# Attention with rotary positions and a token and channel mixer: table loads on ScalarE's queue, the first pair's rotation in two parts with its first head written from PSUM, and 128-partition transposes of the tail rows

## The chip, the cores and the metric

The kernel runs on one core of a Trainium2 chip. The metric is the device time of one execution in microseconds. A core has five engines that run their own in-order queues: TensorE (PE; its weight loads are listed as PEld), VectorE (DVE), ScalarE (ACT), GpSimd (POOL) and SyncE (SP), the last of which issues the DMA transfers. PSUM is the memory that PE writes its results to.

## The reference

Inputs q, k and v are 4 x 8 x 576 x 64 in fp32 (batch, heads, positions, head width). Then come two mixers with residual sums.

```python
def rotate(x):
    x1, x2 = (x[..., :half], x[..., half:])
    return np.concatenate([x1 * cos - x2 * sin, x1 * sin + x2 * cos], axis=-1)
q_rot, k_rot = (rotate(q), rotate(k))
scores = scale * np.matmul(q_rot, k_rot.transpose(0, 1, 3, 2))
attn = softmax(scores)
x = concat_heads(np.matmul(attn, v))               # 4 x 576 x 512
h = np.maximum(x.T @ w_tok1, 0.0) @ w_tok2         # mixes the 576 positions, width 256
u = x + h.T
out = u + np.maximum(u @ w_ch1, 0.0) @ w_ch2       # mixes the 512 channels, width 1536
```

(softmax and concat_heads stand for the reference's lines.) The four weights are float64; the kernel converts them on the chip.

## The kernel before

**Number format.** A matmul takes operands in a format of fewer bits than fp32, so each operand is split into a high part (a copy that rounds, on ACT) and a low part (the fp32 value less the high part, on DVE or POOL), and a product is made of three passes: high by high, high by low, low by high. In attention the two parts of q are stacked on the 128 partitions (head width 64, twice), so that one matmul against the k high part that stands on both halves, and one against the k low part, give all of it.

**Attention.** The 32 combinations of batch and head go two heads at a time, as 16 pairs n. `prep(n)` (L245) makes a pair's operands: load k, q and v (`ld`, `ldt`, L254 to L259; 512 rows as 128 partitions of 4 rows, and the 64 tail rows as a fifth row R on 64 partitions); rotate k and q in four element-wise operations each (`rot`, L286 to L298: times sine, times cosine, and two half-width additions; pair 0 on DVE, the others on POOL); transpose on PE in two groups g into a PSUM tile (`tr`, L317 to L321: rows 0 and 1, then rows 2 and 3 and the tail, which is a 64 x 64 transpose at L321); copy the high part (`fh`, L325, ACT) and subtract the low part (`fl`, L328, DVE); and duplicate each head's parts on both partition halves by DMA over SP (`dup`, L340: eight for k, four for q). v is copied and split by two POOL operations (L272, L275). Four small POOL casts (L365) make a block-diagonal operand for the tail rows of q. The tables of cosines and sines are loaded in two halves over SP: the half for k first of all (L233), the half for q behind pair 0's k (L265).

`pair(n)` (L375) works off nine score tiles: four row tiles of head 0, the tail tile of both heads (L403), and four row tiles of head 1. For each: score matmuls (L412), the row maximum (L417, DVE), the exponential with its row sum (L427, ACT), transposes (L437 and L467, PE), their high parts (ACT, L442, L473) and low parts (DVE, L446, L476). After certain tiles nine matmuls with v follow (L491), and the two halves of the result are added (L494, L497). At a pair's end the result is transposed back (L524, L527) and scaled (L536, L543).

Beside this, `tok_weights` (L619) splits the token mixer's weights in six blocks through `f64_split` (L556): ACT makes a scaled absolute value and the low word's value (L576, L578), then a clamp (L580), a shift (L582), two mask operations (L584, L586), a product and a sum (L588, L590), the high part (L596) and the low part (L597). Clamp, product, sum and low part may go to DVE or POOL, whichever the planner thinks will end first; the rest of the integer work is DVE's.

**Mixers.** Once attention has ended, the token mixer (`tokens`, L668) runs for the four batches while seven blocks of the channel mixer's first weight group are split (`weights`, L732); then the channel mixer (L765, L789) runs four weight groups over six chunks of rows, and the next group's 7 blocks are split beside it.

**What sets the order.** No instruction is issued as it is written. Each is a task of class `Plan` (L56) with an engine, a modelled duration, the tasks that it depends on, the buffers that it takes, and a priority. `Plan.run` (L88) is a list scheduler: it keeps a modelled clock per engine, and of the tasks that can start earliest (within `SLACK`, L144, of the first) it takes the one with the lowest priority. The order in which tasks are picked is the order of each engine's queue on the chip, and it isn't changed there. Priorities are a position (9 n for pair n, plus the tile's number) plus an offset by kind of task out of `AT` (L143). The modelled durations are one-line formulas such as

```python
def pool1(n):
    return n * 0.00115 + 0.07
```

which is the clamp on POOL for n columns; on DVE the planner takes 0.0016 n + 0.05 for it.

Of the kernel before, what the change touches and what calls it, by code (L numbers as in the profile page):

```python
# [142 lines left out]
AT = {"qk": -21.76, "mx": 12.19, "ex": -0.31, "tr": 2.41, "eh": 3.13, "el": 11.77, "tt": -13.32, "th": -37.34, "tl": -11.54, "pv": -15.55, "p1": -1.22, "p2": -8.32, "fin": 13.39, "f6": 9.56, "load": -2.28, "rot": 8.1, "pt": -7.21, "dup": -7.81, "vs": -7.11}  # L143
SLACK = {"PE": 0.16, "ACT": 0, "DVE": 0.16, "POOL": 0, "SP": 0.46}  # L144
# [14 lines left out]
def pool1(n):  # L159
    return n * 0.00115 + 0.07  # L160
# [7 lines left out]
def rope_attention_mixer_kernel(ctx: ExitStack, tc: tile.TileContext, q, k, v, w_tok1, w_tok2, w_ch1, w_ch2, tab, out):  # L168
# [8 lines left out]
    nc = tc.nc  # L177
# [26 lines left out]
    def attention(ctx):  # L204
# [28 lines left out]
        nc.sync.dma_start(out=tabs[:, 0:2], in_=tab[0:2].rearrange("a p r d -> p a r d"))  # L233
# [11 lines left out]
        def prep(n):  # L245
            b, hp = divmod(n, HP)
            pos = 9 * n
            hb = {}
            for nm, src, pr in (("k", k, 0.0), ("q", q, 0.5), ("v", v, 1.0)):
# [14 lines left out]
                if nm == "k" and n == 0:  # L264
                    add("SP", 0.5, lambda: nc.sync.dma_start(out=tabs[:, 2:4], in_=tab[2:4].rearrange("a p r d -> p a r d")),  # L265
                        prio=pos + AT["load"])
                n5 = 2 * (R + 1) * D
                if nm == "v":
                    vb = Buf(vss)

                    def v1(e, rb=rb, vb=vb):
                        return lambda: e.tensor_copy(out=vb.t[:, :, :, 0:D], in_=rb.t.rearrange("p h r d -> p r h d"))  # L272

                    def v2(e, rb=rb, vb=vb):
                        return lambda: e.tensor_tensor(out=vb.t[:, :, :, D:2 * D], in0=rb.t.rearrange("p h r d -> p r h d"),  # L275
                                                       in1=vb.t[:, :, :, 0:D], op=ALU.subtract)

                    x = add("POOL", 0.74, v1(nc.gpsimd), l, [rb, vb], pos + AT["vs"])
# [7 lines left out]
                def rot(e, i, rb=rb, ub=ub, wb=wb, c=c):  # L286
                    def go():
                        src = rb.t.rearrange("p h r d -> p r h d")
                        bc = lambda j: tabs[:, j].unsqueeze(2).to_broadcast([P, R + 1, 2, D])
                        u, w = i and ub.t, i != 1 and wb.t  # L290
# [11 lines left out]
                for i in range(4):  # L302
                    w = n5 if i < 2 else n5 // 2
                    bufs = [[rb, wb], [rb, ub], [ub, wb], [ub, wb]][i]
                    if n == 0:
                        x = [add("DVE", dve(w), rot(nc.vector, i), x, bufs, pos + AT["rot"] + pr)]
                    else:
                        x = [add("POOL", pool(w), rot(nc.gpsimd, i), x, bufs, pos + AT["rot"] + pr)]
                hi, lo = Buf(hls[nm + "h"]), Buf(hls[nm + "l"])
                hb[nm] = (hi, lo)  # L310
                eh, el = [], []
                for g in range(2):
# [4 lines left out]
                    def tr(g=g, tb=tb, ub=ub):  # L317
                        for j, r in enumerate((0, 1) if g == 0 else (2, 3)):
                            nc.tensor.transpose(tb.t[:, j * P:(j + 1) * P], ub.t[:, r].rearrange("p h d -> p (h d)"), ident)  # L319
                        if g == 1:  # L320
                            nc.tensor.transpose(tb.t[:, 2 * P:2 * P + TL], ub.t[0:TL, R].rearrange("p h d -> p (h d)"),  # L321
                                                ident[0:TL, 0:TL])
# [8 lines left out]
                    x2 = add("PE", 0.15 * (2 + g) + 0.1 * g, tr, x, [tb, ub], pp)  # L331
# [12 lines left out]
                if nm == "k":  # L344
                    out_b = [Buf(khds), Buf(klds)]
                    done = {0: [], 1: []}
                    for h in range(2):
# [5 lines left out]
                else:  # L353
                    qb = Buf(qss)
                    done = {0: [], 1: []}
                    for h in range(2):
# [541 lines left out]
```

## Time and profile before

| | us |
|---|---|
| median of 3 runs (lowest to highest) | 728.04 (727.44 to 730.86) |
| the profiled execution | 726.98 |
| its span, from first to last instruction | 725.2 |
| PE busy | 667.1 (92% of the span) |
| DVE busy | 524.3 (72%) |
| ACT busy | 373.8 (52%) |
| POOL busy | 346.1 (48%) |

Busy time is summed over the records of an engine; matmuls are pipelined, so a busy PE is not PE at its peak. A group's line names the kernel's line, the engine, the operation, and its output and inputs by the names of the program's tiles without their numbers: `kh` and `kl` are k's high and low parts, `khd`, `kld` and `qs` the duplicated operands, `s` the scores, `p` the exponentials, `pt` their transposed parts, `t` a PSUM tile, `fa`, `fh` and `fc` the scratch of the weight split. Times in a timeline are microseconds from the span's start.

### The profile page before, as it was taken

How to read it: one execution, taken by the hardware profiler on the slowest of the kernel's cores; microseconds unless marked ns; L12 is line 12 of the kernel's file. 1: busy time of each engine (PE TensorE's matmuls, PEld its weight loads, DVE VectorE, ACT ScalarE, POOL GpSimd, SP SyncE). 2: the span in 40 equal slices, each digit the busy share in tenths (PEclk: the TensorE clock that was granted, in tenths of full speed). 3: DMA queues.
4: the chain of work that ended last, by engine and by line, in shares of the span. 5: the costliest groups of instructions: out<-in, count | busy, mean ns of one | idle time of the engine just before them, and what ended most of it. 6: DMA issues, size and time to landing. Idle time of an engine off the chain costs nothing.

```text
span 725.2 us, 11584 instructions
## 1 busy us (share of the span) xinstructions
PE 667.1 (92%) x3960; PEld 589.3 (81%) x3960; DVE 524.3 (72%) x919; ACT 373.8 (52%) x911; POOL 346.1 (48%) x352
## 2 busy tenths in 40 slices
PE   1698899999999999996948999999999999999997
PEld 0677788788889888885826898989899998989896
DVE  5799999999999999996897588644883375232322
ACT  2588889888888888884552253322431141101110
POOL 4899889788777777302880045121750161000000
PEclk9999999999999999997977999999999999999999
DMA  7575555545555555420220013011220010001122
GB/s 207 163 210 131 129 146 146 137 122 146 145 141 138 146 144 140 99 88 0 81 73 23 0 53 101 23 51 33 70 74 0 5 56 0 1 1 44 58 73 87
DMA packets 45914, 63.14 MB, mean 87 GB/s; under 512 B 13984, under 2 KB 27040, under 8 KB 45856
## 3 DMA queue, kind: packets, MB, share of 16 engines
q1 hardware_dynamic: 45856, 62.41, 31.9%
q8 instruction: 31, 0.51, 0.3%
q14 instruction: 27, 0.22, 0.1%
HBM read 30.41 MB, written 4.72 MB: 48 GB/s over the span
## 4 chain that ended last, share of the span: by engine, by line
PE 70%; DVE 13%; ACT 5%; POOL 4%; issue 4%; DMA 2%; SPq 1%; ACTq 0%; DVEq 0%; POOLq 0%
PE m L779 21%; PE m L802 21%; PE t L491 8%; PE s L412 6%; PE t L437 4%; PE m L717 3%; DVE nm L417 3%; DVE pt L446 2%; PE s L403 2%; ACT p L427 2%; PE t L319 1%; PE t L467 1%; PE m L695 1%; PE t L524 1%; DVE pt L476 1%
## 5 line engine op out<-in xcount | busy, mean ns | idle before, releaser
L781 ACT ACTIVATE gh<-m 128x384 fp32r<-128x384 f32 x72 | 35.3, 491 | 176.6 <-PE m L779 159.2
L427 ACT ACTIVATE p<-s,nm 128x576 f32<-128x576 f32 x144 | 108.0, 750 | 17.2 <-DVE nm L417 16.1
L417 DVE TENSOR_REDUCE nm<-s 128x1 f32<-128x576 f32 x144 | 107.7, 749 | 6.4 <-PE s L412 4.7
L446 DVE TENSOR_TENSOR pt<-t,pt 128x512 fp32r<-128x512 f32 (+1 forms) x160 | 97.3, 628 | 2.4 <-ACT pt L442 1.3
L779 PE MATMUL m<-uh,c1h 128*128 128x384 f32 x288 | 96.7, 336 | 0.0
L779 PE MATMUL m<-uh,c1l 128*128 128x384 f32 x288 | 96.6, 336 | 0.0
L779 PE MATMUL m<-ul,c1h 128*128 128x384 f32 x288 | 96.6, 335 | 0.0
L491 PE MATMUL t<-pt,vs 128*128 128x256 f32 (+1 forms) x576 | 88.7, 298 | 4.4 <-DVE pt L446 1.4
L783 DVE SCALAR_TENSOR_TENSOR gl<-m,gh 128x384 fp32r<-128x384 f32 x72 | 39.8, 556 | 70.7 <-ACT gh L781 70.6
L580 POOL TENSOR_SCALAR fa<-fa 128x512 f32<-128x512 f32 (+3 forms) x34 | 60.0, 1767 | 59.9 <-ACT fa L576 54.4
L491 PEld LDWEIGHTS t<-pt,vs 128*128 128x128 f32 x576 | 79.5, 188 | 8.5 <-ACT p L427 3.6
L437 PE MATMUL t<-ident,p 128*128 128x128 f32 x576 | 84.5, 277 | 1.9 <-DVE oT L497 0.7
L802 PE MATMUL m<-c2h,gl 128*128 128x512 f32 x216 | 85.1, 394 | 0.0
L802 PE MATMUL m<-c2l,gh 128*128 128x512 f32 x216 | 85.0, 393 | 0.0
L802 PE MATMUL m<-c2h,gh 128*128 128x512 f32 x216 | 84.8, 393 | 0.0
L442 ACT CAST pt<-t 128x512 fp32r<-128x512 f32 (+1 forms) x160 | 82.9, 550 | 3.4 <-PE t L437 2.1
L412 PE MATMUL s<-khd,qs 128*128 128x288 f32 x256 | 81.0, 332 | 3.3 <-ACT p L427 1.8
L804 DVE TENSOR_TENSOR X<-m,X 128x512 f32<-128x512 f32 x64 | 43.6, 688 | 49.4 <-PE m L802 49.4
L412 PE MATMUL s<-kld,qs 128*128 128x288 f32 x256 | 72.6, 298 | 0.0
L437 PEld LDWEIGHTS t<-ident,p 128*128 128x128 f32 x576 | 64.7, 140 | 8.5 <-DVE pt L446 2.5
L412 PEld LDWEIGHTS s<-khd,qs 128*128 128x128 f32 x256 | 48.9, 191 | 12.3 <-ACT p L427 9.1
L779 PEld LDWEIGHTS m<-ul,c1h 128*128 128x128 f32 x288 | 54.1, 188 | 0.9
(120 smaller groups left out, 1351.6 us busy)
## 6 DMA issues: line engine op xcount, KB each, us to landing
khd<-kh SPq DMA_DIRECT2D x64, 144.0 KB, 2.5
kld<-kl SPq DMA_DIRECT2D x64, 144.0 KB, 2.7
stg<-in_moe_w_ch_dram SPq DMA_DIRECT2D x16, 384.0 KB, 3.1
stg<-in_moe_w_ch_dram SPq DMA_DIRECT2D x12, 512.0 KB, 3.5
kraw<-in_k_dram SPq DMA_DIRECT2D x16, 256.0 KB, 2.9
qraw<-in_q_dram SPq DMA_DIRECT2D x16, 256.0 KB, 3.0
vraw<-in_v_dram SPq DMA_DIRECT2D x16, 256.0 KB, 2.9
qs<-qh SPq DMA_DIRECT2D x32, 128.0 KB, 2.5
```

Of the source, the lines that this page charges most:

```text
L412: nc.tensor.matmul(sb.t[:, c, 0:W2], a, m.t[:, h, c * W2:(c + 1) * W2], start=(x == 0), stop=(x == 1))
L417: nc.vector.tensor_reduce(out=nm.t, in_=sb.t[:, :, 0:W2], axis=AX.XY, op=ALU.max, negate=True)
L427: nc.scalar.activation(out=p.t.rearrange("p (a b) -> p a b", a=2), in_=sb.t[:, :, 0:W2], func=ACTF.Exp, bias=nm.t, accum_out=l)
L437: nc.tensor.transpose(tb.t[:, j * P:(j + 1) * P], p.t[:, j * P:(j + 1) * P], ident)
L442: nc.scalar.copy(out=pt[c].t[:, 0:R, d0:d0 + w], in_=tb.t.rearrange("p (j q) -> p j q", j=R)[:, :, s0:s0 + w])
L446: nc.vector.tensor_tensor(out=pt[c].t[:, R + 1:2 * R + 1, d0:d0 + w], in0=tb.t.rearrange("p (j q) -> p j q", j=R)[:, :, s0:s0 + w], in1=pt ...
L491: nc.tensor.matmul(ab.t[:, 0:w], vb.t[:, r, h], pt[c].t[:, j, 0:w], start=(x == 0), stop=(x == 2 * R))
L580: clamp = lambda e: lambda: e.tensor_scalar(out=A(), in0=A(), scalar1=EXP_LO, scalar2=EXP_HI, op0=ALU.max, op1=ALU.min)
L779: nc.tensor.matmul(tb.t[:, 0:N], a, m, start=(i == 0), stop=(i == len(lst) - 1))
L783: y = add("DVE", 0.56, lambda f=f, tb=tb: nc.vector.scalar_tensor_tensor(out=gb.t[1][:, f], in0=tb.t[:, 0:N], scalar=0.0, in1=gb.t[0][:, f ...
L802: nc.tensor.matmul(tb.t, a, m, start=(i == 0), stop=(i == len(lst) - 1))
L804: y = add("DVE", 0.69, lambda u=u, tb=tb: nc.vector.tensor_tensor(out=u, in0=tb.t, in1=u, op=ALU.add), [z] + sums.get((ci, x), []), [tb], ...
```

## The change

Five things change.

1. Both halves of the tables are loaded by ScalarE's DMA queue, the first instructions on it; SP begins with k.
2. Pair 0's rotation of k and q on DVE is made in two parts, rows 0 and 1 and then rows 2, 3 and the tail, each of four operations. The first transposes wait for the first part only.
3. For pair 0 and head 0 the duplicated parts are written straight from the PSUM tile of the transposes: high parts by ACT (`ch`), low parts by DVE (`cl`), to both partition halves for k and one each for q. The six DMA duplications of head 0 are left out; the plain high and low copies stay, as head 1 and the tail need them. These tasks have priorities near -60 (`FIRST`).
4. The tail rows' transpose, of every pair, takes all 128 partitions (the lower 64 hold zeros) and writes 128 columns, of which 64 are read.
5. The planner: all offsets in `AT` are new, `SLACK` is zero but for SP, the modelled clamp on POOL costs 0.004 n + 0.07, k's and q's transposes 0.13 (2 + g). v's POOL tasks now depend on the end of the pair's k and q rotations.

```diff
-AT = {"qk": -21.76, "mx": 12.19, "ex": -0.31, "tr": 2.41, "eh": 3.13, "el": 11.77, "tt": -13.32, "th": -37.34, "tl": -11.54, "pv": -15.55, "p1": -1.22, "p2": -8.32, "fin": 13.39, "f6": 9.56, "load": -2.28, "rot": 8.1, "pt": -7.21, "dup": -7.81, "vs": -7.11}
-SLACK = {"PE": 0.16, "ACT": 0, "DVE": 0.16, "POOL": 0, "SP": 0.46}
+AT = {"qk": -30.7, "mx": 30.06, "ex": -2.13, "tr": 1.27, "eh": -10.75, "el": 15.57, "tt": -24.59, "th": -29.34, "tl": -21.22, "pv": -7.19, "p1": -4.38, "p2": -3.09, "fin": 15.37, "f6": -15.84, "load": 0.72, "rot": -5.73, "pt": -7.68, "dup": -17.69, "vs": -36.1}
+FIRST = -60.0
+SLACK = {"PE": 0, "ACT": 0, "DVE": 0, "POOL": 0, "SP": 0.18}
...
 def pool1(n):
-    return n * 0.00115 + 0.07
+    return n * 0.004 + 0.07
...
-        nc.sync.dma_start(out=tabs[:, 0:2], in_=tab[0:2].rearrange("a p r d -> p a r d"))
+        nc.scalar.dma_start(out=tabs[:, 0:2], in_=tab[0:2].rearrange("a p r d -> p a r d"))
+        nc.scalar.dma_start(out=tabs[:, 2:4], in_=tab[2:4].rearrange("a p r d -> p a r d"))
...
-                if nm == "k" and n == 0:
-                    add("SP", 0.5, lambda: nc.sync.dma_start(out=tabs[:, 2:4], in_=tab[2:4].rearrange("a p r d -> p a r d")),
-                        prio=pos + AT["load"])
...
-                    x = add("POOL", 0.74, v1(nc.gpsimd), l, [rb, vb], pos + AT["vs"])
+                    x = add("POOL", 0.74, v1(nc.gpsimd), l + last, [rb, vb], pos + AT["vs"])
...
+                part = []
+                for r0, r1 in ((0, 2), (2, R + 1)) if n == 0 else ((0, R + 1),):
+                    for i in range(4):
+                        w = (r1 - r0) * 2 * D // (1 if i < 2 else 2)
+                        bufs = [[rb, wb], [rb, ub], [ub, wb], [ub, wb]][i]
+                        if n == 0:
+                            x = [add("DVE", dve(w), rot(nc.vector, i, r0=r0, r1=r1), x, bufs, FIRST + pr + r0)]
+                        else:
+                            x = [add("POOL", pool(w), rot(nc.gpsimd, i), x, bufs, pos + AT["rot"] + pr)]
+                    part.append(x)
+                last += x
...
                         if g == 1:
-                            nc.tensor.transpose(tb.t[:, 2 * P:2 * P + TL], ub.t[0:TL, R].rearrange("p h d -> p (h d)"),
-                                                ident[0:TL, 0:TL])
+                            nc.tensor.transpose(tb.t[:, 2 * P:3 * P], ub.t[:, R].rearrange("p h d -> p (h d)"), ident)
...
-                    x2 = add("PE", 0.15 * (2 + g) + 0.1 * g, tr, x, [tb, ub], pp)
+                    x2 = add("PE", 0.13 * (2 + g), tr, part[min(g, len(part) - 1)], [tb, ub], pp if n else FIRST + g)
+                    if n == 0:
+
+                        d = qb if nm == "q" else out_b[0]
+                        w0 = min(w, M - c0) if nm == "q" else w
+
+                        def ch(o, tb=tb, d=d, c0=c0, w0=w0):
+                            return lambda: nc.scalar.copy(out=d.t[o * D:(o + 1) * D, 0, c0:c0 + w0], in_=tb.t[0:D, 0:w0])
+
+                        def cl(o, tb=tb, d=d, c0=c0, w0=w0, z=qb if nm == "q" else out_b[1]):
+                            return lambda: nc.vector.tensor_tensor(out=z.t[o * D:(o + 1) * D, 0, c0:c0 + w0], in0=tb.t[0:D, 0:w0],
+                                                                   in1=d.t[0:D, 0, c0:c0 + w0], op=ALU.subtract)
+                        y = add("ACT", act(w0), ch(0), [x2], [tb, d], FIRST + g)
+                        direct.append(y)
+                        if nm == "k":
+                            direct.append(add("ACT", act(w0), ch(1), [x2], [tb, d], FIRST + g))
+                            direct += [add("DVE", dve(w0), cl(o), [y], [tb, d, out_b[1]], FIRST + g) for o in range(2)]
+                        else:
+                            direct.append(add("DVE", dve(w0), cl(1), [y], [tb, d], FIRST + g))
...
-                    done = {0: [], 1: []}
-                    for h in range(2):
+                    done = {0: direct, 1: []}
+                    for h in range(n == 0, 2):
```

(The last hunk stands twice, for k and for q. `rot` takes r0 and r1 and slices its operands by them.)

More of the change, by code (lines that the diff above doesn't have):

```diff
@@ L248, in prep @@
             hb = {}
+            last = []
             for nm, src, pr in (("k", k, 0.0), ("q", q, 0.5), ("v", v, 1.0)):
@@ L284, in prep, with rot @@
                 hd = D // 2
-                def rot(e, i, rb=rb, ub=ub, wb=wb, c=c):
+                def rot(e, i, rb=rb, ub=ub, wb=wb, c=c, r0=0, r1=R + 1):
                     def go():
-                        src = rb.t.rearrange("p h r d -> p r h d")
-                        bc = lambda j: tabs[:, j].unsqueeze(2).to_broadcast([P, R + 1, 2, D])
-                        u, w = i and ub.t, i != 1 and wb.t
+                        src = rb.t.rearrange("p h r d -> p r h d")[:, r0:r1]
+                        bc = lambda j: tabs[:, j, r0:r1].unsqueeze(2).to_broadcast([P, r1 - r0, 2, D])
+                        u, w = i and ub.t[:, r0:r1], i != 1 and wb.t[:, r0:r1]
                         if i == 0:
@@ L301, in prep @@
                 x = l
[L302 to L308, printed above, removed]
+                part = []
[9 more added lines that the diff above has]
+                last += x
                 hi, lo = Buf(hls[nm + "h"]), Buf(hls[nm + "l"])
                 hb[nm] = (hi, lo)
-                eh, el = [], []
+                eh, el, direct = [], [], []
+                if nm == "k":
+                    out_b = [Buf(khds), Buf(klds)]
+                else:
+                    qb = Buf(qss)
                 for g in range(2):
@@ L330, in prep @@
                     pp = pos + AT["pt"] + pr + 0.2 * g
-                    x2 = add("PE", 0.15 * (2 + g) + 0.1 * g, tr, x, [tb, ub], pp)
+                    x2 = add("PE", 0.13 * (2 + g), tr, part[min(g, len(part) - 1)], [tb, ub], pp if n else FIRST + g)
[9 more added lines that the diff above has]
+                        direct.append(y)
+                        if nm == "k":
+                            direct.append(add("ACT", act(w0), ch(1), [x2], [tb, d], FIRST + g))
+                            direct += [add("DVE", dve(w0), cl(o), [y], [tb, d, out_b[1]], FIRST + g) for o in range(2)]
+                        else:
+                            direct.append(add("DVE", dve(w0), cl(1), [y], [tb, d], FIRST + g))
                     x3 = add("ACT", act(w), fh, [x2], [tb, hi], pp)
@@ L344, in prep @@
                 if nm == "k":
-                    out_b = [Buf(khds), Buf(klds)]
-                    done = {0: [], 1: []}
-                    for h in range(2):
+                    done = {0: direct, 1: []}
+                    for h in range(n == 0, 2):
                         for z, src in ((0, hi), (1, lo)):
@@ L353, in prep @@
                 else:
-                    qb = Buf(qss)
-                    done = {0: [], 1: []}
-                    for h in range(2):
+                    done = {0: direct, 1: []}
+                    for h in range(n == 0, 2):
                         for o, src in ((0, hi), (1, lo)):
```

## The prediction

> **What bounds the kernel now.** I began with the page's chain of work that ended last, then read busy time by stretch. In the rows below the columns are the stretch, its length, busy time of PE, PEld, DVE, ACT and POOL (with counts), granted clock, DMA share and GB/s. The stretches are: first pair's preparation, pairs 0 and 1, pairs 1 to 7 (beside which six blocks of token weights are split), pairs 8 to 15, the passage into the mixers, and the channel mixer.
>
> ```profile
> PE 70%; DVE 13%; ACT 5%; POOL 4%; issue 4%; DMA 2%; SPq 1%; ACTq 0%; DVEq 0%; POOLq 0%
> ```
> ```profile
> 5.00:23.00 18.00, 3.05 (x11) 2.05 (x12) 12.04 (x17) 3.24 (x7) 11.85 (x12) 1.00 0.78 217
> 23.00:47.00 24.00, 22.12 (x143) 18.96 (x142) 20.57 (x38) 18.92 (x50) 20.70 (x21) 1.00 0.59 158
> 47.00:168.00 121.00, 111.20 (x804) 97.99 (x803) 115.83 (x220) 104.19 (x270) 104.68 (x112) 1.00 0.56 143
> 187.00:317.00 130.00, 128.05 (x945) 115.00 (x945) 123.48 (x240) 113.69 (x303) 86.36 (x103) 1.00 0.56 140
> 346.00:386.00 40.00, 26.48 (x111) 20.20 (x111) 36.91 (x48) 19.73 (x37) 30.56 (x20) 0.82 0.26 77
> 420.00:725.00 305.00, 300.56 (x1519) 272.22 (x1517) 154.19 (x249) 70.02 (x140) 67.77 (x48) 1.00 0.14 43
> ```
>
> The channel mixer is PE alone (300.56 of 305), and nothing of the change can gain there. Pairs 8 to 15 press PE (128.05 of 130) with DVE close behind (123.48, 95.0%). Pairs 1 to 7 press DVE (115.83 of 121, 95.7%), with POOL at 86.5%. The passage is DVE's too (36.91 of 40). Only the first stretch has an idle PE and a DVE that is idle a third of the time. The pace of the pairs shows in the tail tile, one per pair, here of pairs 1, 7, 9 and 15 (start, duration, engine, line, operation):
>
> ```profile
> 47.05 0.54 PE L403 MATMUL s<-kh,bd 128*128 128x288 f32 x2
> 168.24 0.53 PE L403 MATMUL s<-kh,bd 128*128 128x288 f32 x2
> 205.64 0.50 PE L403 MATMUL s<-kh,bd 128*128 128x288 f32 x2
> 316.65 0.50 PE L403 MATMUL s<-kh,bd 128*128 128x288 f32 x2
> ```
>
> Pairs 1 to 7 take 121.2 / 6 = 20.2 us each, pairs 9 to 15 111.0 / 6 = 18.5 us. Next the timeline of the start, in order of time, where a bracket gives idle time and its releaser:
>
> ```profile
> 0.73 0.44 SPq L233 DMA_DIRECT2D tabs<-in_tab_dram  x1
> 1.22 0.46 SPq L255 DMA_DIRECT2D kraw<-in_k_dram  x1
> 2.52 0.59 SPq L265 DMA_DIRECT2D tabs<-in_tab_dram  x1
> 5.63 0.82 DVE L292 TENSOR_TENSOR w<-kraw,tabs 128x640 f32<-128x640 f32 x1 [5.63 <-DMA kraw<-in_k_dram]
> 7.63 0.49 DVE L298 TENSOR_TENSOR uk<-uk,w 128x320 f32<-128x320 f32 x1
> 9.36 0.42 DVE L328 TENSOR_TENSOR kl<-t,kh 128x256 fp32r<-128x256 f32 x1 [0.39 <-ACT kh L325]
> 9.70 2.14 DVE L294 TENSOR_TENSOR uq<-qraw,tabs 128x640 f32<-128x640 f32 x1
> 11.77 0.48 DVE L328 TENSOR_TENSOR kl<-t,kh 128x320 fp32r<-128x320 f32 x1
> 13.10 1.12 PE L319 MATMUL t<-ident,uq 128*128 128x128 f32 x4 [3.46 <-DVE uq L298]
> 13.83 0.37 ACT L325 CAST qh<-t 128x256 fp32r<-128x256 f32 x1 [3.72 <-PE t L319]
> 14.86 1.91 POOL L580 TENSOR_SCALAR fa<-fa 128x512 f32<-128x512 f32 x1 [0.19 <-ACT fa L576]
> 16.69 0.54 SPq L340 DMA_DIRECT2D qs<-ql  x1
> 16.80 0.43 DVE L582 TENSOR_SCALAR fa<-fa 128x512 uint32<-128x512 uint32 x1 [1.19 <-POOL fa L580]
> 17.27 0.69 DVE L584 SCALAR_TENSOR_TENSOR fh<-stg,fa 128x512 uint32<-128x512 uint32 x1
> 18.00 0.43 DVE L586 TENSOR_SCALAR fa<-fh 128x512 uint32<-128x512 uint32 x1
> 18.53 0.69 DVE L588 TENSOR_TENSOR fa<-fc,fa 128x512 f32<-128x512 f32 x1
> 19.26 1.90 DVE L590 TENSOR_TENSOR fh<-fh,fa 128x512 f32<-128x512 f32 x1
> 22.74 0.69 PE L319 MATMUL t<-ident,uk 128*128 128x128 f32 x2 [8.23 <-POOL uk L298]
> 23.08 0.59 PE L412 MATMUL s<-khd,qs 128*128 128x288 f32 x1
> ```
>
> The first score matmul starts at 23.08, after twelve head copies by DMA (the last for head 0 issued at 16.69), and behind two transposes of pair 1's k, which PE had queued ahead of it and for which it sat 8.23 us on POOL.
>
> **The first pair.** Two table transfers leave SP, so kraw is issued at 0.73 in place of 1.22, and the tail piece with it: DVE could start at 5.63 - 0.49 = 5.1. The second table now travels beside kraw. I take 5.3, and 6.4 as the far end (second table in front). The Trainium skill, "DMA: Bandwidth & Descriptors", on issuing engines not being separate DMA queues, says that both queues share the same engines and interleave, so that only issue time is saved; by it the start would be 5.14 at best and perhaps no earlier than now, a difference of half a microsecond in the sum.
>
> Rotation: 640 columns take 0.82 and 320 take 0.49, so 1.03 ns per column and 0.16 us fixed. A tensor in two parts costs 2 x (0.42 + 0.29 + 0.56 + 0.36) = 3.26 in place of 2.62; both 6.5 us. That uq op of 2.14 ran beside POOL's v work, which now waits for the last rotation, so I count it at its plain price. The direct low parts are six DVE ops, four of 256 columns (0.42) and two of 320 (0.48), 2.6 us; ACT's six copies (about 0.4 each) hide beside DVE, as do the untouched high and low copies for head 1. Of those DVE ops all but the last come before or between the rotations: 5.3 + 6.5 + 2.2 = 14.0. Then two transposes and their latency (13.10 to 13.83: 0.7), a copy (0.4), the last low part (0.4), and 0.4 for a plain low copy in the way: 16.0. So the first score matmul comes 7.1 us earlier. Ends: 14.5 without extra DVE work in front (-8.6), 18 with the late tables and pair 1's transposes again queued ahead (-5.1). Six of twelve DMA copies go from SP; behind a wait of POOL's v task stand pair 1's rotations, which can't start sooner than kraw's second load anyway.
>
> **What the gap had hidden.** In 16.80 to 21.16 DVE did 4.1 us of the first weight block in the gap. With scores from 16 on, it competes with pair 0. Price 0 (DVE had 3.4 us idle in 23 to 47) to +4.1; I take +1.5.
>
> **The clamps.** The planner's price of a clamp on POOL goes from 0.66 to 2.12 us for 512 columns, beside 0.87 on DVE; so nearly all move to DVE. On POOL they took, in the weight phase and in the passage (stretch, length, POOL busy, count, clock, DMA, GB/s):
>
> ```profile
> 14.00:168.00 154.00, 9.62 (x6) 1.00 0.58 150
> 336.00:384.00 48.00, 12.98 (x7) 0.78 0.23 66
> ```
>
> The trace has no float clamp on DVE. The nearest rows are the integer shift behind it (L582) and the mask (L586), both one-source ops of the same widths; DVE busy, L582 first, then L586:
>
> ```profile
> 14.00:168.00 154.00, 5.18 (x6) 1.00 0.58 150
> 336.00:384.00 48.00, 7.60 (x7) 0.78 0.23 66
> 14.00:168.00 154.00, 4.23 (x6) 1.00 0.58 150
> 336.00:384.00 48.00, 3.71 (x7) 0.78 0.23 66
> ```
>
> L582 follows a POOL op and often meets the next one; L586 follows DVE, as the clamp nearly will (it follows ACT). I take L586: +4.2 in the weight phase, +3.7 in the passage; ends are the 0.43 of a free op and L582's mean. The Trainium skill, "SBUF — State Buffer", section on who interferes with whom, says that a one-source DVE op in a two-port mode and a POOL op lock each other out of a shared port pair, the later one blocking fully; the 0.43 at 16.80 against L582's mean of 0.86 agrees, and by it a clamp would cost 0.43 plus the rest of a POOL op, near L582's price.
>
> POOL is freed by 9.6 and 13.0 us. In the weight phase I count only the clamp at 14.86, which stood before pair 1's rotation: -1.9 (0 to -9.6). In the passage L582 averages 7.60 / 7 = 1.09, which is 3.9 more in all than L586: such waits stand in DVE's time there, on the other two-operand lines too, and the clamps are over a third of POOL's work. I take 4.1 off for all of them: net -0.4 (-4 to +4). In the mixer the clamps lie under PE.
>
> **The tail transposes.** Pair 9's are typical:
>
> ```profile
> 208.78 0.38 PE L319 MATMUL t<-ident,uq 128*128 128x128 f32 x2
> 209.10 0.27 PE L321 MATMUL t<-ident,uq 64*128 64x64 f32 x1
> 209.30 0.66 PE L437 MATMUL t<-ident,p 128*128 128x128 f32 x4
> PEld t L321 <- issue: 5.9, 32, 0.3
> ```
>
> Full transposes start 0.11 apart, so the follower would start at 209.11 in place of 209.30: 0.19 saved, 32 times 6.1 in all (5.9 us of idle weight loads says the same). It pays where PE leads, pairs 8 to 15: 16 x 0.19 = 3.0, and DVE at 95% there takes some back. I take -2.2 (0 to -6.1). The new offsets reorder every engine; no row prices that. I take 0, with DVE's idle time in 187 to 317, 6.5 us, to either side.
>
> **Sum.** -7.1 + 1.5 + 4.2 - 1.9 - 0.4 - 2.2 = -5.9. The profiled execution took 726.98 (725.2 of span), so 721.1; the median shown, 728.04, stands 1.06 above it: 722.1.
>
> **Rivals.** (a) All of the start carries through: block 0 fits in pair 0's holes, clamps cost a free 0.43 or less each (+2.2 in the weight phase), POOL's relief gives half its 9.6, the passage gains 4 and the pairs 2.2: -7.1 + 2.2 - 4.8 - 4 - 2.2 = -15.9, so 712. For it: POOL rows stand in the early chain; against it: DVE at 95.7%.
>
> (b) DVE's budget eats the start. From 5 to 168 it is busy 12.04 + 20.57 + 115.83 = 148.4; the change adds 1.3 (parts), 2.6 (direct), 4.2 (clamps) and saves 1.3: 155.2. At its present 95.7% that is 162.2 us, from 5.3 to 167.5: 0.5 gained. With -2.2 and -0.4: 725. My sum needs 97.4%, more than DVE has in any of these stretches, which speaks for (b); but the weight blocks may slide to later pairs.
>
> (c) Slower: the clamps as a DVE stall. Place: the two phases in which DVE leads. If each of their 13 clamps waits as L582 does in the passage (1.09), they cost 14.1 with no relief, DVE then also holds the tail's gain: -7.1 + 1.5 + 14.1 = +8.5, so 736.5. It decides from a mean of (7.1 - 1.5) / 13 = 0.43 us without relief, and shows beyond noise from 0.71. The skill's lock rule above would speak for it; that POOL's load falls speaks against.
>
> (d) The change doesn't do what it says: the planner again puts pair 1's transposes ahead of the first score, which then starts near 21, 5 us later than I have it: 722.1 + 5 = 727.
>
> **Chances.** Forecast 0.46 (717 to 727 alone), (a) 0.24, (b) with (d) 0.19, (c) 0.11. A measurement of this kernel can tell about 0.5%, 3.6 us. Faster than 724.4: three quarters of the forecast, all of (a) and a little of (b), 0.61. Within: the rest of these, 0.28; slower than 731.7: 0.11. Range: (a) with a better order reaches 709; (c) half-way is 731.
>
> **What would show it.** The first score matmul at 14.5 to 18 with no pair-1 transpose ahead; no POOL row for the clamp, and a DVE row of 0.4 to 1.1 us; tail transposes without the issue wait, and pairs 9 to 15 at 18.2 to 18.4 us; pair 7's tail tile at 163 to 168; the first long run of channel matmuls earlier by about 6. I am wrong if pairs 1 to 7 slow by over 0.6 us each, or if the new order moves the 18.5 us of a late pair by more than 0.4.

## The result

The changed kernel takes 711.19 us (median of 4 runs, 709.06 to 712.31) where the kernel before took 728.48 beside it: a ratio of 0.9755 (95% interval 0.9719 to 0.979), 17.3 us faster. A second comparison, five rounds on another occasion, gave 0.9743 (0.972 to 0.9766). The forecast was 722.1 us, 6 us faster, so the direction was right and the forecast gain was about a third of the measured one. 711.2 lies inside the stated range, 0.8 us from the 712 of rival (a), but, as the runs show, hardly for the reasons of (a).

The profiled execution has a span of 706.9 us, 18.3 less than before. The first view is the timeline of the start, as before: start and duration in us, engine, line and operation. (Lines of `kernel.py` have moved: score matmuls are L435, the tail tile L426, the clamp L603, the shift behind it L605.)

```profile
5.00 0.43 DVE L292 TENSOR_TENSOR w<-kraw,tabs 128x256 f32<-128x256 f32 x1 [5.00 <-DMA tabs<-in_tab_dram]
...
13.61 2.21 POOL L603 TENSOR_SCALAR fa<-fa 128x512 f32<-128x512 f32 x1 [11.07 <-ACT fa L599]
16.79 1.65 POOL L292 TENSOR_TENSOR w<-kraw,tabs 128x640 f32<-128x640 f32 x1 [0.30 <-DVE uq L298]
16.96 1.77 DVE L603 TENSOR_SCALAR fa<-fa 128x512 f32<-128x512 f32 x1
17.31 0.59 PE L435 MATMUL s<-khd,qs 128*128 128x288 f32 x1
19.58 1.10 DVE L607 SCALAR_TENSOR_TENSOR fh<-stg,fa 128x512 uint32<-128x512 uint32 x1
20.61 1.41 DVE L440 TENSOR_REDUCE nm<-s 128x1 f32<-128x576 f32 x2
21.94 1.60 DVE L609 TENSOR_SCALAR fa<-fh 128x512 uint32<-128x512 uint32 x1
23.46 1.08 DVE L605 TENSOR_SCALAR fa<-fa 128x512 uint32<-128x512 uint32 x1
```

The first scores come at 17.31 in place of 23.08, as the change says. But their maximum waits until 20.61 behind DVE's own queue, and weight operations follow. Here is the stretch from the first scores to pair 1's tail tile, before and then after (stretch, length, busy time of PE, PEld, DVE, ACT and POOL with counts, granted clock, DMA share, GB/s):

```profile
23.08:47.05 23.97, 22.09 (x143) 18.88 (x141) 20.62 (x38) 18.97 (x51) 20.67 (x21) 1.00 0.59 158
```
```profile
17.31:52.27 34.96, 25.22 (x162) 22.41 (x161) 32.76 (x52) 23.49 (x60) 29.42 (x31) 1.00 0.56 147
```

DVE is busy 12 us more in it, most of it with weights, whose lines take 1.7 us of DVE there before and 12.1 us after. The next rows are the tail tiles of pairs 0, 1, 7, 9 and 15:

```profile
27.12 0.82 PE L426 MATMUL s<-kh,bd 128*128 128x288 f32 x2 [0.42 <-ACT p L450]
52.27 0.51 PE L426 MATMUL s<-kh,bd 128*128 128x288 f32 x2
168.61 0.46 PE L426 MATMUL s<-kh,bd 128*128 128x288 f32 x2
204.24 0.47 PE L426 MATMUL s<-kh,bd 128*128 128x288 f32 x2
311.27 0.43 PE L426 MATMUL s<-kh,bd 128*128 128x288 f32 x2
```

Against before (29.11, 47.05, 168.24, 205.64, 316.65) pair 0 is 2.0 us early, pair 1 5.2 us late, and pair 7 0.4 us late: nothing of the earlier first scores is left. (Pairs 1 to 7 take 19.39 us each in place of 20.20, which wins back most of what pair 1 had lost.) Pairs 9 to 15 then take 107.03 / 6 = 17.84 us each in place of 18.50, and pair 15 is 5.4 us early. The last view of this section gives the end of attention (its last scaling on POOL) and the first channel matmul, in the kernel before and then in the changed one:

```profile
336.00 1.04 POOL L543 TENSOR_TENSOR X<-X,ri 128x512 f32<-128x512 f32 x1 [5.41 <-ACT X L533]
420.45 0.42 PE L779 MATMUL m<-uh,c1h 128*128 128x384 f32 x1
```
```profile
328.99 1.04 POOL L566 TENSOR_TENSOR X<-X,ri 128x512 f32<-128x512 f32 x1 [5.06 <-ACT X L556]
402.09 0.42 PE L802 MATMUL m<-uh,c1h 128*128 128x384 f32 x1
```

Attention ends 7.0 us earlier. The passage from that scaling to the first channel matmul falls from 84.4 to 73.1 us, by 11.3. What follows takes 304.8 us in both. So the account is about 0 up to pair 7 (0.4 lost), 7.4 from there to the end of attention, and 11.3 from the passage.

### The profile page after: what moved, and what is told of

Same layout as the page of the kernel before. It is cut to its first block, busy times and chain, and to the rows that moved or that the text cites. A ratio compares the mean times of both kernels' runs of the same rounds, so it can differ in the third digit from the quotient of the medians.

```text
span 706.9 us, 11543 instructions
## 1 busy us (share of the span) xinstructions
PE 656.4 (93%) x3960; PEld 588.2 (83%) x3960; DVE 520.4 (74%) x938; ACT 378.1 (53%) x917; POOL 331.9 (47%) x347
## 4 chain that ended last, share of the span: by engine, by line
PE 56%; DVE 26%; ACT 7%; issue 5%; POOL 2%; DMA 2%; DVEq 0%; SPq 0%; ACTq 0%; POOLq 0%
PE m L802 21%; PE m L825 21%; DVE nm L440 8%; DVE pt L469 6%; PE t L514 4%; ACT pt L465 2%; PE s L435 2%; DVE oT L520 2%; DVE pt L499 2%; ACT p L450 2%; PE m L740 2%; PE t L460 1%; POOL xs L701 1%; PE m L718 1%; PE t L547 1%
## 5 line engine op out<-in xcount | busy, mean ns | idle before, releaser
L514 PE MATMUL t<-pt,vs 128*128 128x256 f32 (+1 forms) x576 | 92.2, 304 | 4.0 <-DVE pt L469 1.6
L435 PE MATMUL s<-khd,qs 128*128 128x288 f32 x256 | 81.9, 336 | 9.7 <-ACT p L450 7.9
L514 PEld LDWEIGHTS t<-pt,vs 128*128 128x128 f32 x576 | 78.8, 189 | 10.4 <-DVE pt L469 4.0
L460 PEld LDWEIGHTS t<-ident,p 128*128 128x128 f32 x576 | 67.7, 142 | 7.2 <-DVE pt L499 3.2
L435 PE MATMUL s<-kld,qs 128*128 128x288 f32 x256 | 72.5, 299 | 0.0
L435 PEld LDWEIGHTS s<-khd,qs 128*128 128x128 f32 x256 | 49.1, 192 | 17.6 <-ACT p L450 13.8
L802 PEld LDWEIGHTS m<-uh,c1h 128*128 128x128 f32 x288 | 54.1, 188 | 0.9
```

The lines of the kernel that those rows point to most:

```text
L435: nc.tensor.matmul(sb.t[:, c, 0:W2], a, m.t[:, h, c * W2:(c + 1) * W2], start=(x == 0), stop=(x == 1))
L460: nc.tensor.transpose(tb.t[:, j * P:(j + 1) * P], p.t[:, j * P:(j + 1) * P], ident)
L514: nc.tensor.matmul(ab.t[:, 0:w], vb.t[:, r, h], pt[c].t[:, j, 0:w], start=(x == 0), stop=(x == 2 * R))
L802: nc.tensor.matmul(tb.t[:, 0:N], a, m, start=(i == 0), stop=(i == len(lst) - 1))
```

## The experiments

Below, "late pairs" is the mean of pairs 9 to 15, from tail tile to tail tile, and "passage" is counted from the start of the last scaling. (The expectation of the first run counts it from the scaling's end and has 83.6 and 72.3; by the rows above these are 83.4 and 72.1.) The theories: the clamps' move to DVE, the tail transposes, the new order of tasks, and the start.

### One part alone, on the kernel before

The clamp's price:

```diff
-    return n * 0.00115 + 0.07
+    return n * 0.004 + 0.07
```

> The kernel before with one edit: the planner's price of the clamp on POOL is 0.004 n + 0.07. If the clamps explain the passage (it took 83.6 us from the last scaling at 337.0 to the first channel matmul at 420.7 before, and 72.3 after the change), the passage falls to 73 to 77 us and the total to 717 to 721 us. If it is the new order of tasks (offsets and slack) that shortened the passage, it stays at 81 to 85 us and the total at 725 to 732 us. By the prediction's own term (-0.4 us in the passage, +2.3 us in the weight phase) the total is 729 to 731 us.

Measured: 725.26 us, ratio 0.9957 (0.9941 to 0.9974); passage 82.0, late pairs 18.46. The clamps are worth 2.4 us of the passage, and not 11.

The tail transposes, every queue in the order of before:

```diff
-    nc.tensor.transpose(tb.t[:, 2 * P:2 * P + TL], ub.t[0:TL, R].rearrange("p h d -> p (h d)"),
-                        ident[0:TL, 0:TL])
+    nc.tensor.transpose(tb.t[:, 2 * P:3 * P], ub.t[:, R].rearrange("p h d -> p (h d)"), ident)
```

> The kernel before with one edit: the tail rows are transposed with 128 partitions; the planner's prices are left, so every queue has the order of before. The late pairs took 18.50 us each before and 17.82 us after the change. If the transposes give all of that, they fall to 17.8 to 17.9 us and the total to 719 to 723 us. By the slot arithmetic of the prediction (two slots of 0.19 us a pair) they take 18.1 us and the total is 723 to 725 us. If DVE at 95% holds the pairs, they stay above 18.35 us and the total within 2 us of before.

Measured: 727.81 us, ratio 0.9995 (0.998 to 1.001); late pairs 18.58. They give nothing. Pairs 9 to 15, first in the kernel before and then in this run, by stretch as above:

```profile
205.64:316.65 111.01, 109.33 (x808) 98.33 (x808) 105.39 (x206) 97.09 (x260) 72.46 (x87) 1.00 0.56 140
```
```profile
206.63:318.14 111.51, 107.37 (x808) 98.12 (x808) 105.53 (x206) 96.94 (x260) 72.44 (x87) 1.00 0.55 140
```

PE is busy 2.0 us less, and the six pairs take 0.5 us more. Here are the waits of the weight loads between 205 and 316 us (engine, tile and line, what it waited for; us in total, times, longest), first of the kernel before:

```profile
PEld s L412 <- ACT p L427: 2.5, 11, 0.2
PEld t L321 <- issue: 2.0, 12, 0.2
...
PEld t L524 <- DVE ql L328: 1.3, 6, 0.2
```

and of this run, whose lines stand one lower:

```profile
PEld s L411 <- ACT p L426: 4.0, 13, 1.3
PEld t L523 <- DVE ql L327: 2.8, 6, 0.5
...
PEld s L402 <- issue: 1.3, 4, 0.3
```

The 2.0 us of issue wait at the transposes are gone, and the scores and the final transposes wait 3.0 us more for ACT's exponentials and DVE's low parts. (Of the smaller rows, 1.1 us of the scores' wait for `pt` is gone too.) PE did less and waited more; its busy time did not set the pace.

Offsets and slack together:

```diff
-AT = {"qk": -21.76, "mx": 12.19, "ex": -0.31, ...
-SLACK = {"PE": 0.16, "ACT": 0, "DVE": 0.16, "POOL": 0, "SP": 0.46}
+AT = {"qk": -30.7, "mx": 30.06, "ex": -2.13, ...
+SLACK = {"PE": 0, "ACT": 0, "DVE": 0, "POOL": 0, "SP": 0.18}
```

> The kernel before with the new offsets and the new slack, nothing else. If the new order is what makes the late pairs shorter, they fall from 18.50 us to below 18.2 us; if it is the transposes, they stay at 18.4 to 18.6 us. The mixers' tasks have no offsets, only the slack and the clocks at their start are new for them: if the passage's gain is the slack's, it falls from 83.6 us to below 76 us and the total to 715 to 720 us; if it is the clamps', it stays above 81 us and the total is 725 to 731 us.

Measured: 729.4 us, ratio 1.0016 (0.9999 to 1.0032). Attention became slower: pair 7's tail tile stands at 174.8 in place of 168.2, so most of the loss comes before it, the late pairs take 18.88, and the last scaling is at 343.8 in place of 336.0. The passage became shorter by 7.6 (76.8). One gain and one loss cancel.

### The change without its start

The kernel before with the planner's numbers and the tail transposes of the change, but tables over SP, the rotation whole, twelve DMA copies, and v not waiting (the diff is against the changed kernel and shows some of its lines):

```diff
-        nc.scalar.dma_start(out=tabs[:, 0:2], in_=tab[0:2].rearrange("a p r d -> p a r d"))
-        nc.scalar.dma_start(out=tabs[:, 2:4], in_=tab[2:4].rearrange("a p r d -> p a r d"))
+        nc.sync.dma_start(out=tabs[:, 0:2], in_=tab[0:2].rearrange("a p r d -> p a r d"))
...
-                    x = add("POOL", 0.74, v1(nc.gpsimd), l + last, [rb, vb], pos + AT["vs"])
+                    x = add("POOL", 0.74, v1(nc.gpsimd), l, [rb, vb], pos + AT["vs"])
...
-                    for h in range(n == 0, 2):
+                    for h in range(2):
```

> The changed kernel without its edits to the start: tables over SP, first pair's rotation whole, head 0 duplicated by DMA, v not waiting for the rotations; tail transposes, offsets, slack and prices as changed. The changed kernel's tail tile of pair 7 stands at 168.6 us against 168.2 us before, so if the start's gain was eaten by the weight phase whatever the start is, the total stays at 710 to 714 us. If the start's 7 us are in the result and something else lost them, the total is 716 to 720 us.

Measured: 711.81 us, ratio 0.9768 (0.9735 to 0.98); late pairs 17.87, passage 72.8. The result is there without the start, within what the runs scatter.

### Undoing one part of the changed kernel

The tail transposes with 64 partitions again, in the changed kernel's order:

```diff
-    nc.tensor.transpose(tb.t[:, 2 * P:3 * P], ub.t[:, R].rearrange("p h d -> p (h d)"), ident)
+    nc.tensor.transpose(tb.t[:, 2 * P:2 * P + TL], ub.t[0:TL, R].rearrange("p h d -> p (h d)"),
+                        ident[0:TL, 0:TL])
```

> The changed kernel with the tail rows transposed by 64 partitions as before; the planner's prices are left, so every queue has the changed kernel's order. The late pairs took 17.84 us each in the changed kernel, and 18.88 us in the run with the new offsets and slack alone. If the 128-partition transposes are worth that whole us a pair under the new offsets, the late pairs take 18.6 to 18.9 us and the total is 722 to 730 us. If they are worth two slots of 0.19 us, 18.1 to 18.3 us and 714 to 719 us. If they are worth nothing, as under the old order, and the new order with its lower price of the transposes makes the difference, 17.8 to 17.9 us and 710 to 713 us.

Measured: 708.56 us, ratio 0.9729 (0.9707 to 0.975), late pairs 17.82. That seemed even a little faster, so both were run once more side by side:

> The changed kernel once more, beside the same kernel with 64-partition tail transposes, to tell 711.2 us from 708.6 us on one chip. If the transposes with 128 partitions are worth their two slots of 0.19 us a pair, this one is 3 to 6 us faster than the other; if they are worth nothing, as under the old order, the two agree within 2 us; if 64 partitions are the better form, this one is 2 to 3 us slower.

> The changed kernel with 64-partition tail transposes, as run before at 708.6 us: within 2 us of the changed kernel if the form of the transposes is worth nothing, 3 to 6 us above it by the slot arithmetic, 2 to 3 us below it if the first comparison was no chance.

Measured: 709.28 us with 128 partitions (0.9743, 0.972 to 0.9766) and 710.29 with 64 (0.9757, 0.9732 to 0.9781). The two can't be told apart. The transposes are worth nothing that can be measured, in either order.

The old price of the clamp on POOL:

```diff
-    return n * 0.004 + 0.07
+    return n * 0.00115 + 0.07
```

> The changed kernel with the old price of the clamp on POOL, so that the planner puts the clamps on POOL again. Alone this price took 2.4 us off the passage (84.4 to 82.0 us from the last scaling to the first channel matmul) and 2.5 us off the total. If it adds up, the passage goes from 73.1 to 75 to 77 us and the total is 713 to 716 us. If the clamps' place matters more with the new order (DVE leads there), the total is over 717 us; if the order has made it irrelevant, 709 to 713 us.

Measured: 714.94 us, ratio 0.9814 (0.9784 to 0.9844); passage 76.2, late pairs 17.93. The move of the clamps is worth 3 us of the passage and 4 to 6 us of the total (against 711.19 and 709.28). The rest of it lies in attention: pair 7's tail tile stands at 172.1 here and at 168.6 in the changed kernel.

The planner's old offsets, slack and clamp price, with the start, the transposes and their price as changed:

```diff
-AT = {"qk": -30.7, "mx": 30.06, "ex": -2.13, ...
-SLACK = {"PE": 0, "ACT": 0, "DVE": 0, "POOL": 0, "SP": 0.18}
+AT = {"qk": -21.76, "mx": 12.19, "ex": -0.31, ...
+SLACK = {"PE": 0.16, "ACT": 0, "DVE": 0.16, "POOL": 0, "SP": 0.46}
...
-    return n * 0.004 + 0.07
+    return n * 0.00115 + 0.07
```

> The changed kernel with the old offsets, the old slack and the old clamp price: tables, first pair, tail transposes and v's wait as changed. If the start's edits can pay under the old order, pair 7's tail tile comes 4 to 7 us before 168.2 us and the total is 720 to 724 us. If DVE's budget up to pair 7 eats them in any order, pair 7's tail tile stays at 166 to 170 us, the late pairs at 18.4 to 18.6 us, and the total at 725 to 730 us.

Measured: 726.87 us, ratio 0.9983 (0.9966 to 1.0). First scores at 16.45, pair 7's tail tile at 170.0, late pairs 18.49, passage 84.1. The new code without the planner's new numbers is worth nothing that can be measured.

### Which of the planner's numbers

All the new slack alone (the offsets of before):

```diff
-SLACK = {"PE": 0.16, "ACT": 0, "DVE": 0.16, "POOL": 0, "SP": 0.46}
+SLACK = {"PE": 0, "ACT": 0, "DVE": 0, "POOL": 0, "SP": 0.18}
```

> The kernel before with the new slack alone. The new offsets and the new slack together shortened the passage from 84.4 to 76.8 us, though no offset belongs to a task of the passage. If the slack did it, the passage is 75 to 79 us here; if it is the state in which attention ends (the engines' modelled clocks, the last pair's order), it stays at 82 to 86 us.

Measured: 731.28 us, ratio 1.0041 (1.0027 to 1.0054): passage 76.9, but late pairs 18.80 and the last scaling at 348.8. Then DVE's slack alone at zero, and PE's alone:

```diff
-SLACK = {"PE": 0.16, "ACT": 0, "DVE": 0.16, "POOL": 0, "SP": 0.46}
+SLACK = {"PE": 0.16, "ACT": 0, "DVE": 0, "POOL": 0, "SP": 0.46}     # DVE's alone
+SLACK = {"PE": 0, "ACT": 0, "DVE": 0.16, "POOL": 0, "SP": 0.46}     # PE's alone
```

> The kernel before with the slack of DVE alone set to zero. All three new slacks together took the passage from 84.4 to 76.9 us. In the passage before, PE sat 8.4 us on ACT's c2h copy, which waits for DVE's weight work, while token work stood behind it: if DVE's slack let weight operations go ahead of the token mixer's, the passage is 75 to 79 us here. If it was PE's or SP's slack, 82 to 86 us.

> The kernel before with the slack of PE alone set to zero. If PE's slack made the order of the passage, it is 75 to 79 us here and 82 to 86 us with DVE's slack alone at zero; if neither alone does it, both stay above 80 us and the gain is one of a whole order that no single slack owns.

Measured: with DVE's 726.81 us (0.9985, 0.997 to 1.0001) and a passage of 77.1; with PE's 740.83 us (1.0177, 1.0153 to 1.0201) and a passage of 84.3. So DVE's slack is what made the passage long. What it gives there it loses in attention (last scaling at 345.4, late pairs 19.03). The whole passage by stretch, of the kernel before, with DVE's slack at zero, and of the changed kernel:

```profile
336.00:420.40 84.40, 67.56 (x303) 53.35 (x304) 66.28 (x98) 32.81 (x67) 36.35 (x24) 0.85 0.13 38
345.40:422.40 77.00, 68.30 (x303) 53.84 (x304) 63.20 (x93) 32.63 (x66) 43.04 (x30) 0.89 0.14 42
329.00:402.10 73.10, 65.22 (x305) 50.27 (x305) 63.87 (x96) 32.88 (x67) 36.79 (x26) 0.98 0.14 44
```

PE stands idle 16.8 us before, 8.7 with DVE's slack at zero and 7.9 in the changed kernel. Of the 11.3 us, 9.0 are shorter waits; the other 2.3 are PE's busy time. (The granted clock is 0.85 before and 0.98 in the changed kernel; with DVE's slack at zero it is 0.89 and PE is busy 68.3 us, so the clock is not what took the 7.4 us off there.) The waits of PE's matmuls in the passage, of the kernel before:

```profile
PE m L695 <- ACT c2h L596: 8.4, 1, 8.4
PE m L695 <- DVE xs L678: 6.0, 2, 4.6
PE m L695 <- DVE xs L676: 2.4, 1, 2.4
PE m L695 <- POOL xs L678: 0.5, 1, 0.5
```

with DVE's slack at zero:

```profile
PE m L695 <- DVE xs L678: 4.0, 2, 2.6
PE m L717 <- DVE ul L760: 2.7, 2, 2.0
PE m L695 <- DVE xs L676: 2.5, 1, 2.5
```

and of the changed kernel:

```profile
PE m L718 <- DVE xs L699: 2.2, 1, 2.2
PE m L718 <- DVE xs L701: 1.7, 2, 1.0
PE m L718 <- DVE ul L783: 1.6, 1, 1.6
PE m L740 <- DVE rs L726: 1.5, 1, 1.5
```

The single wait of 8.4 us, in which token matmuls sat and which the profile puts down to ACT's copy of a channel weight, is gone in both. Before, PE waited 17.3 us in these rows; with DVE's slack at zero 9.2. The timeline before shows what stood in the way:

```profile
375.22 0.60 ACT L700 ACTIVATE rs<-m 128x512 fp32r<-128x512 f32 x1 [0.26 <-PE m L695]
382.18 0.69 DVE L590 TENSOR_TENSOR fh<-fh,fa 128x512 f32<-128x512 f32 x1
382.79 1.28 DVE L703 SCALAR_TENSOR_TENSOR rs<-m,rs 128x512 fp32r<-128x512 f32 x2
383.62 1.20 PE L695 MATMUL m<-xs,w1h 128*128 128x512 f32 x2 [8.44 <-ACT c2h L596]
```

The token mixer's high parts `rs` are done at 375.82, but their low parts on DVE (L703) start at 382.79, behind nine weight operations, the last of them at 382.18. They read the PSUM tiles `m`, whose buffers, by the program, the next token matmuls need; the copy of the channel weight is no operand of theirs. So I put the wait down to DVE's queue and not to the copy.

With the slack at zero the late pairs are slower, under the old offsets (18.80) as under the new (18.88), and yet they take 17.84 us in the changed kernel. One number was left, the planner's price of k's and q's transposes:

```diff
-    x2 = add("PE", 0.15 * (2 + g) + 0.1 * g, tr, x, [tb, ub], pp)
+    x2 = add("PE", 0.13 * (2 + g), tr, x, [tb, ub], pp)
```

> The kernel before with the new offsets, the new slack and the planner's new price of k's and q's transposes, 0.13 (2 + g) for 0.15 (2 + g) + 0.1 g; the transposes themselves, the clamp's price and the start as before. With offsets and slack alone the late pairs took 18.88 us, in the changed kernel 17.84 us, and neither the 128-partition transposes nor the clamp's price nor the start made the difference there. If the price of the transposes is the missing piece, the late pairs take 17.8 to 18.0 us and the total is 713 to 718 us. If it needs the clamp's price as well, they stay above 18.6 us and the total above 724 us.

Measured: 717.87 us, ratio 0.9856 (0.9838 to 0.9873); late pairs 17.86, passage 76.3. And taken back in the changed kernel:

> The changed kernel with the planner's old price of k's and q's transposes, all else as changed. If that price decides the order of the late pairs, they go from 17.84 us to 18.6 to 18.9 us and the total to 722 to 730 us; if it doesn't, they stay below 18.0 us and the total at 708 to 713 us.

Measured: 724.46 us, ratio 0.9939 (0.9923 to 0.9955); late pairs 18.98, passage 73.0. So a modelled 0.04 us on a task of two transposes and 0.16 us on one of three decide over a microsecond a pair, and 11.5 us of the total where the price is added and 13.3 us where it is taken back (15.2 against the second measurement of the changed kernel). Not all of it is the late pairs' 6 to 7 us: pair 7's tail tile moves by 2.5 us in the one case (174.8 to 172.4) and by 6.7 in the other (168.6 to 175.3). (Up to there the granted clock is 0.95 with the old price and 1.00 without it in the profiled executions; but at a mean clock of 0.99 over the run the two kernels took 724.6 and 712.3 us, so the clock is not the cause.) Busy time from pair 9's to pair 15's tail tile (stretch, length, then PE, PEld, DVE, ACT, POOL), first with the old price, then of the changed kernel:

```profile
213.08:326.95 113.87, 107.63 (x806) 98.61 (x805) 105.24 (x205) 98.51 (x259) 72.95 (x87) 1.00 0.53 137
```
```profile
204.24:311.27 107.03, 104.58 (x806) 98.83 (x805) 103.63 (x206) 98.33 (x259) 72.94 (x87) 1.00 0.57 145
```

The work is the same (806 matmuls, 259 ACT operations, DVE within 1.6 us). DVE is busy 92.4% of the time with the one and 96.8% with the other. The waits say where part of the rest went, first with the old price, then of the changed kernel:

```profile
PEld s L435 <- ACT p L450: 5.6, 12, 0.5
PEld t L514 <- DVE pt L469: 5.3, 12, 0.6
...
DVE nm L440 <- ACT p L450: 2.4, 5, 0.5
```
```profile
PEld s L435 <- ACT p L450: 2.5, 6, 0.4
```

With the old price the matmuls with v are queued just where DVE's low parts aren't ready, twice a pair; in the changed kernel that wait has no row.

### Can the start pay?

The changed kernel with the six weight blocks held back: their loads wait for the first exponential of a pair.

```diff
+                marks.setdefault(n, x)
...
+        at = iter((0, 2, 4, 6, 8, 10))      # in the other kernel 2, 3, 4, 5, 6, 7
...
-    pr = pos()
-    sb, t = stage(0, w1v[:, i * 512:(i + 1) * 512], pr)
+    pr, after = pos(), [marks[next(at)]]
+    sb, t = stage(0, w1v[:, i * 512:(i + 1) * 512], pr, deps=after)
```

> The changed kernel with one more dependence: the loads of the six token weight blocks wait for the first exponential of pairs 0, 2, 4, 6, 8 and 10, so that their splits are spread over more pairs. In the changed kernel the first scores came 5.8 us earlier but pair 1's tail tile 5.2 us later than before, with two weight blocks split by DVE beside pair 0. If that early weight work is what eats the start's gain, the step from pair 0's to pair 1's tail tile falls from 25.2 to 18 to 21 us and the total to 703 to 708 us. If DVE's whole budget holds, the blocks only cost later what they cost now: 708 to 713 us.

> As the kernel with spread blocks, but the loads wait for pairs 2, 3, 4, 5, 6 and 7, so that pairs 0 and 1 have no weight work beside them. If weight work delays pair 1, its tail tile comes at 44 to 47 us in place of 52.3 us; whether the total falls below 708 us says if DVE has room for the blocks later. If pair 1 waits for POOL's rotation whatever the weights do, its tail tile stays at 49 to 53 us.

Measured: 729.6 us (1.0026, 1.0008 to 1.0044) and 728.78 us (1.0004, 0.9988 to 1.0021). With weights from pair 2 on, pair 1's tail tile came at 44.77, against 52.27 in the changed kernel and 47.05 before: weight work beside pairs 0 and 1 is what delays pair 1. With blocks at even pairs, of which one is beside pair 0, it came at 51.39; but DVE is busy only 27.2 of the 34.3 us from the first scores to there, so DVE's weight work alone doesn't explain this delay, and its cause stays open (the granted clock is 0.95 there). Neither kernel kept anything: pair 7's tail tile stood at 178.6 in the first and 180.9 in the second, and the late pairs took 18.35 and 18.22 us. The passage was 73.3 and 72.9 us, as in the changed kernel, so the whole loss is in attention. Holding back six blocks changed the order of everything behind them, and so these two runs don't say what the start would be worth in an order as good as the changed kernel's.

## Why the prediction was right or wrong

**The step that failed** is the last term before the sum: "The new offsets reorder every engine; no row prices that. I take 0." It was put at nothing with a bound (6.5 us to either side) for the late pairs only, and at nothing without a bound for the passage. The runs show that the planner's numbers, the fifth point of the change and no part of the title, are nearly all of the result: with the start undone the kernel takes 711.81 us, and with the old offsets, slack and clamp price under all the new code 726.87. What follows takes the terms one by one.

**The first pair (-7.1).** First scores came at 17.31, inside 14.5 to 18, with no transpose of pair 1 in front, 5.8 us earlier and not 7.1. DVE began at 5.00 (5.3 predicted, 6.4 the far end), so the second table delayed nothing against the 5.1 that I had without it; its start was released by a table, no longer by k's tail. ACT's copies didn't hide beside DVE: four times, at 7.90, 8.76, 12.02 and 13.00, DVE stood idle before a direct low part until a copy of ACT had ended, 2.3 us in all. What failed here is the step behind it, "What the gap had hidden" (+1.5, at most +4.1). From pair 0's to pair 1's tail tile it took 25.15 us, not 17.94: 7.2 us lost. DVE's weight work from the first scores to there is 10.4 us more than before, where I had 4.1 at most. Two blocks were being split from the start (clamps at 13.61 and 16.96) and a third began at 47.45, and the first maximum stood 3.3 us behind the first scores, against 1.35 before. Pairs 1 to 7 then won 4.9 us back.

**Rival (b), DVE's budget,** had the right time for this half: 155.2 us of DVE work from 5 to 168 us, and an end of pair 7 within 0.5 us of before.

```profile
5.00:168.00 163.00, 136.23 (x960) 120.74 (x961) 153.20 (x292) 130.51 (x333) 131.68 (x141) 1.00 0.57 147
```

It is 153.2 us, 94.0% of the time, and pair 7 is 0.4 us late. My own sum needed 97.4% there and said so, and I kept it all the same; that step was wrong. But that the budget is the mechanism isn't shown, and one run speaks against it: with the six clamps beside the pairs all back on POOL, which takes 3.8 us of them from DVE, pair 7's tail tile comes at 172.1, 3.5 us later and not earlier. The 0.4 us are a sum of gains and losses. With the planner's offsets, slack and price of transposes alone pair 7 stands at 172.4 (4.1 late), with the clamps' price and the tail transposes too at 169.6, and with the start at 168.6. So the start carries about 1 us to there, and none of it can be told in the total (711.81 without it).

**The clamps (+4.2 - 1.9, and -0.4 in the passage).** Their own cost was nearly right. 26 of 34 went to DVE, so the sign "no POOL row for the clamp" missed; four of them take 3.80 us on DVE between 5 and 168 us, and six take 3.29 us in the passage (I had 4.2 for six and 3.7 for seven). All of them (line, engine, operation, forms, count; busy us, mean ns, then idle before):

```profile
L603 DVE TENSOR_SCALAR fa<-fa 128x512 f32<-128x512 f32 (+2 forms) x26 | 15.6, 603 | 2.0 <-ACT fa L599 1.9
L603 POOL TENSOR_SCALAR fa<-fa 128x384 f32<-128x384 f32 (+2 forms) x8 | 14.7, 1838 | 38.4 <-ACT fa L599 38.4
L605 DVE TENSOR_SCALAR fa<-fa 128x512 uint32<-128x512 uint32 (+3 forms) x34 | 19.8, 586 | 1.3 <-POOL fa L603 1.1
```

The mean of 0.60 us lies where I put it by the mask's row. What was mis-sized is the relief. The shift behind the clamp fell from 0.89 to 0.59 us, 10.4 us over the 34, two thirds of what the 26 clamps cost DVE. I read this as POOL's clamp no longer ending just ahead of it; no run shows it alone. Of the 10.4 us, 2.6 lie in the passage (7.60 to 5.00) and 0.7 beside the pairs (5.18 to 4.47); the rest is in the channel mixer, where PE leads and it gains nothing. The Trainium skill, "SBUF — State Buffer", section on who interferes with whom, has a one-source DVE operation in a two-port mode and a POOL operation lock each other out, the later one for as long as the earlier runs (no row here names the mode). The clamp of 1.77 us at 16.96, which began while POOL ran an operation of 1.65 us from 16.79, agrees with it; the median of 0.41 us shows how often there is no such delay. Rival (c), a clamp that waits each time, was far off. In total the move is worth 2.4 us of the passage alone and 3.1 beside the other changes, against my 0.4. Up to pair 7, where I had 2.3 us lost, it lost 0.5 in the old order and gained 3.5 in the new one (one profile of each; two of the changed kernel differ by 0.5 there).

**The tail transposes (-2.2).** Wrong: 0. The slots went as I read them, the issue wait vanished from the rows, and the pairs kept their pace. I took the bound of the late pairs from PE's 128.05 of 130 busy us. That is a busy time of overlapped matmuls: with the transposes changed it fell by 2.0 us over six pairs and the pairs took no less. DVE's share of the late pairs is 94.9% before and 96.8% in the changed kernel with 1.8 us less work, so another order let it run through. That DVE alone decides is not shown, since PE too is busy over 97% in both. The end of 0 that I gave was the right one.

**The order (0, with 6.5 to either side).** This is the term that held the result. In the passage I gave it nothing and didn't look at the slack, which the diff shows. DVE's slack of 0.16 us let the planner put weight work ahead of the token mixer's; without it the passage is 7.4 us shorter. In the late pairs offsets, slack and the price of the transposes together take 0.64 us off each (18.50 to 17.86), though the first two alone add 0.38. Here the prediction's own test had said that I am wrong if a late pair moves by over 0.4; it moved by 0.66.

**Rival (a)** had the total (712 against 711.2), with a start that carries, freed POOL time and 2.2 us of transposes. Of its terms the start came to nothing that can be told and the transposes to 0; the passage (-4, measured -11.3) had the right sign and about a third of the size. That its sum comes out right is luck: a right number for wrong reasons.

What stays open: why 0.16 us in the price of a transpose task leads to the better order, and why the clamps' move helps up to pair 7 in the one order and not in the other. The rows show which waits go, not by which choice of the planner; and nothing here says that the order found is the best one.

## What to carry to other kernels

Where a planner writes the queues, its constants are part of the kernel: undo them before crediting any edit beside them, for here the code edits were worth nothing that could be measured and four lines of numbers nearly all of the 17 us. Where two engines are both busy some 95% of a stretch, look at the waits between them: here taking 2.0 us from one of them changed nothing, and another order of the same work took 0.66 us off a pair. Before counting on an early start, ask what work the gap used to hide: here that work came to stand beside the first pairs, and holding it back didn't make the start pay either.

## What the runs showed that was not expected

A clamp of two operations on fp32, 512 columns wide, took 1.91 us on POOL before (at 14.86); on DVE, where the median of the thirteen of that width was 0.42 us, it is over four times as fast. The two-operand product behind it is nearer to a factor of two (512 columns on POOL 1.29 us in the mean of seven, and 0.69 on DVE at 18.53). And the issue wait at the 64 x 64 transposes, 5.9 us of idle weight loads over the run, was worth nothing that can be measured when it was removed, in two different orders.
